# A pool of its own for rounded x, small projection buffers kept open, and a last low part in another buffer

## The chip, the cores and the metric

The kernel runs on one core of a Trainium2 chip. The metric is the device time of one execution in microseconds (us). Six engines matter here: TensorE (PE, with its weight loads PEld), ScalarE (ACT), VectorE (DVE), GpSimd (POOL), SyncE (SP, which only issues transfers) and the 16 DMA engines. ScalarE issues transfers too, on a queue of its own (ACTq in the profile).

## What is computed

```python
x = A_x                                             # 1 x 2048 x 640
g = sigmoid((x * gate_w).sum(-1, keepdims=True))
q, k, v = heads(x @ wqkv)                           # 32 heads of 20
a = softmax(q @ k.T * 20 ** -0.5) @ v               # for each head
a = merge(a) @ wo
h = layernorm(x)                                    # over the 640 channels
u = gelu(einsum("bsd,sf->bdf", h, w1) + b1)         # across the 2048 tokens, F = 1728
b = (einsum("bdf,fs->bds", u, w2) + b2).T
out = g * a + (1 - g) * b
```

## The kernel before

All matrix products run in a three-pass form: each float32 operand is split into a rounded high part and the rest (`hi_lo`: the high part by ScalarE, the low part by VectorE or GpSimd), and high x high, high x low and low x high are added up in PSUM.

The program has these stages, one after the other:

1. Projections. `xh` and `xl` hold all of x, transposed, split into high and low: 20 + 20 tiles of 128 x 512 in the pool `p1` at the right side of the memory. `qk_unit(m, w, q)` makes one 128 x 512 piece of q or k: 15 matmuls, then `evh` (high, ScalarE) and `evl` (low, VectorE), which SyncE's queue stores to DRAM (`q_d`, `k_d`). `evh` and `evl` have two buffers each in `p1`, so each waits for the store of the piece two before it. `p1` also holds two buffers `xr` for raw weights and one `kf` for differences of k, used by the first three column blocks of k alone. Between the pieces, the projections of v and the layernorm statistics are made.
2. The token MLP, in two halves of 320 channels. `w_raw(k)` loads a raw block of weights `wr`, `w_split(k)` splits it into `wh` (ScalarE) and `wl` (GpSimd), and TensorE computes `u` and then `y`. The first four blocks are loaded into `p1` and split into two borrowed tiles `wtmp0`, `wtmp1` while the last projections run; raw blocks 4 to 7 are loaded into other borrowed tiles. From block 4 on the split goes to `wh`/`wl` of the pool `gp`, and from block 8 on the raw blocks go to `wr` of `gp`. `gp` is opened when `p1` is closed and takes its place in the memory. Between the matmuls of the MLP run the score tiles `s` of the first pairs of heads (line 199), of which only the row maxima are kept: by `ov` (ScalarE copies a tile with a Relu, line 214) and then a joint maximum (VectorE, line 224), or by a reduction (line 205).
3. Attention (`st`, exp, `pv`), in which ScalarE's exponentials follow each other closely.
4. The output projection and the gate.

The order on TensorE, ScalarE and VectorE is that of the code from the start, and on GpSimd and SyncE's queue from the MLP's preparation on. In the MLP a small planner with a clock of its own (`act`, `later_on`, `settle`, `force`) decides where ScalarE's steps stand among the others; it knows only its own estimates. The first of its steps is the split of block 4.

The loop `for n, (m, q) in enumerate(units)` (lines 513 to 539) walks the last 24 pieces; n = 20 to 23 are the last four of k, `evh9_0` to `evh9_3` and `evl9_0` to `evl9_3`. Behind it comes `p1s.close()`, line 540.

Of the kernel before, what the change touches and what calls it, by code (L numbers as in the profile page):

```python
# [8 lines left out]
F32R = mybir.dt.float32r  # L9
# [4 lines left out]
P = 128  # L14
# [3 lines left out]
NC = D // P  # L18
# [12 lines left out]
def gated_mix(ctx, tc, xT, x, wqk, wv0, wv1, wo, w1, w1t, b1, w2, b2, out):  # L31
# [6 lines left out]
    def hi_lo(hi, lo, src, hi_eng=None, lo_eng=None):  # L38
        if hi_eng is nc.scalar:
            nc.scalar.activation(hi, src, AF.Copy)  # L40
        else:
            (hi_eng or nc.vector).tensor_copy(hi, src)
        (lo_eng or nc.vector).tensor_sub(lo, src, hi.bitcast(F32))  # L43
# [6 lines left out]
    def mm3(ps, pairs):  # L50
        n = len(pairs)
        for i, (ah, al, bh, bl) in enumerate(pairs):
            for k, (a, b) in enumerate(((ah, bh), (ah, bl), (al, bh))):
                nc.tensor.matmul(ps, a, b, start=(i == 0 and k == 0), stop=(i == n - 1 and k == 2))
# [18 lines left out]
    def st_tile(shape, name):  # L73
        n = st_count[0] % 4
        st_count[0] += 1
        return banks[0].tile(shape, F32, tag=f"st{n}", bufs=1, name=name)
# [12 lines left out]
    def q4(shape, dt, name):  # L89
        return base.tile(shape, dt, tag="q4", bufs=6, name=name)  # L90
# [42 lines left out]
    def base_stack(p, full, eng=nc.sync):  # L133
        ks = k8([P, S], F32R, f"ks{p}_{full}")
        qs = [q4([P, S // 2], F32R, f"qs{p}_{full}_{i}") for i in range(2)]
        load_stack(p, ks, qs, full, eng)
        return ks, qs
# [138 lines left out]

    p1s = ExitStack()
    p1 = p1s.enter_context(tc.tile_pool(name="p1", bufs=1, side="right"))
    xh = [[p1.tile([P, 512], F32R, name=f"xh{c}_{q}") for q in range(4)] for c in range(NC)]
    xl = [[p1.tile([P, 512], F32R, name=f"xl{c}_{q}") for q in range(4)] for c in range(NC)]  # L280

    def w_dma(m):
        raw = p1.tile([P, NC, P], F32, tag="xr", bufs=2, name=f"wr{m}")
# [3 lines left out]
    def load_w(m, raw=None):  # L287
        if raw is None:
            raw = w_dma(m)
        wh = q4([P, NC, P], F32R, f"wh{m}")  # L290
        wl = q4([P, NC, P], F32R, f"wl{m}")
        hi_lo(wh, wl, raw, hi_eng=nc.scalar)
        return wh, wl
# [3 lines left out]
    def qk_unit(m, w, q):  # L297
        wh, wl = w
        ps = st_tile([P, 512], f"qk{m}_{q}")
        mm3(ps, [(wh[:, c], wl[:, c], xh[c][q], xl[c][q]) for c in range(NC)])  # L300
        hi = p1.tile([P, 512], F32R, tag="evh", bufs=2, name=f"evh{m}_{q}")
        lo = p1.tile([P, 512], F32R, tag="evl", bufs=2, name=f"evl{m}_{q}")
        hi_lo(hi, lo, ps, hi_eng=nc.scalar)
        c = m - NC
        dst = q_d if m < NC else k_d
        rows = slice((m % NC) * P, (m % NC + 1) * P)
        cols = slice(q * 512, (q + 1) * 512)
        nc.sync.dma_start(dst[0, rows, cols], hi.bitcast(F32))
        nc.sync.dma_start(dst[1, rows, cols], lo.bitcast(F32))
        if not 0 <= c * P < DROWS:  # L310
            return
        if q % 2 == 0:
            k_first[c] = p1.tile([P, 512], F32, tag="kf", bufs=1, name=f"kf{c}_{q}")
            nc.vector.tensor_copy(k_first[c], ps)
            return
        put = nc.gpsimd.dma_start if c < 2 else nc.sync.dma_start
        put(kd_d[0, rows, cols], hi.bitcast(F32))
        put(kd_d[1, rows, cols], lo.bitcast(F32))
        kd = k_first.pop(c)
        nc.vector.tensor_sub(kd, kd, ps)  # L320
        if c == 2:
            dh = p1.tile([P, 512], F32R, tag="evh", bufs=2, name=f"dh{c}_{q}")
        else:
            dh = (pvp if c else px).tile([P, 512], F32R, tag="dh", bufs=1, name=f"dh{c}_{q}")
        hi_lo(dh, kd.bitcast(F32R), kd, hi_eng=nc.scalar)
        cols = slice((q - 1) * 512, q * 512)
        put(kd_d[0, rows, cols], dh.bitcast(F32))
        put(kd_d[1, rows, cols], kd)
# [18 lines left out]
    w = {0: load_w(0, raws[0])}  # L347
    load_x(0)
    w[NC] = load_w(NC, raws[NC])
    for q in range(4):  # L350
        if q < 3:
            load_x(q + 1)
        if q == 1:
            raws[1] = w_dma(1)
        if q == 2:
            w[1] = load_w(1, raws[1])
            raws[NC + 1] = w_dma(NC + 1)
        qk_unit(0, w[0], q)
        qk_unit(NC, w[NC], q)
# [20 lines left out]
    for n in range(8):  # L380
        if 2 <= n < 2 + NC:
            split_wv(0, n - 2)
            load_wv(1, n - 2)
        qk_unit((1, NC + 1)[n // 4], w[(1, NC + 1)[n // 4]], n % 4)
        if n == 0:
            w[NC + 1] = load_w(NC + 1, raws[NC + 1])
# [13 lines left out]
    for half in range(2):  # L400
        wvh, wvl = wvs[half]
        width = HALF + 2 if half == 0 else HALF
        for t in range(NT):
# [11 lines left out]
            q, cols = t // 4, slice((t % 4) * P, (t % 4 + 1) * P)  # L415
# [26 lines left out]
    def h_load(d, t):  # L442
        xm = hp.tile([P, HALF], F32, tag="xm", bufs=4, name=f"xm{d}_{t}")
        nc.sync.dma_start(xm, x[t * P:(t + 1) * P, d * HALF:(d + 1) * HALF])
        xms[d, t] = xm

    def h_norm(d, t):
        xm = xms[d, t]
        (nc.vector if d else nc.gpsimd).tensor_scalar(xm, xm, negm[:, t:t + 1], rstd[:, t:t + 1], op0=OP.add, op1=OP.mult)

    def h_split(d, t):
        xm = xms.pop((d, t))
        a = hp.tile([P, HALF], F32R, tag=f"hh{t}", name=f"hh{d}_{t}")
        b = hp.tile([P, HALF], F32R, tag=f"hl{t}", name=f"hl{d}_{t}")
        hi_lo(a, b, xm, hi_eng=nc.scalar, lo_eng=nc.gpsimd)
        return a, b
# [14 lines left out]
    def w_raw(k):  # L471
        src, _ = w_list[k]
        n, m = src.shape[1], src.shape[2]
        if k < AHEAD:
            raw = p1.tile([P, 4, P], F32, tag="xr", bufs=2, name=f"wr{k}")
        elif k < 2 * AHEAD:
            raw = q4([P, 4, P], F32, f"wr{k}")
        else:
            raw = gp.tile([P, 4, P], F32, tag="wr", bufs=8, name=f"wr{k}")
        (nc.scalar if k < 2 * AHEAD else nc.sync).dma_start(raw[:, :n, :m], src)  # L480
        w_raws.append(raw)

    def w_split(k):
        src, tail = w_list[k]
        raw = w_raws[k]
        n, m = src.shape[1], src.shape[2]
        if k < AHEAD:
            o = 8 * (k % 2)
            hi, lo = w_tmp[k // 2][:, o: o + 4], w_tmp[k // 2][:, o + 4: o + 8]
        else:  # L490
            hi = gp.tile([P, 4, P], F32R, tag="wh", bufs=5, name=f"wh{k}")
            lo = None if tail else gp.tile([P, 4, P], F32R, tag="wl", bufs=5, name=f"wl{k}")
        if tail:
            hi_lo(hi[:, :n, :m], hi[:, :n, m:], raw[:, :n, :m], hi_eng=nc.scalar, lo_eng=nc.gpsimd)
        else:
            hi_lo(hi[:, :n], lo[:, :n], raw[:, :n], hi_eng=nc.scalar, lo_eng=nc.gpsimd)
        w_got[k] = hi, lo
# [15 lines left out]
    for n, (m, q) in enumerate(units):  # L513
        if q == 0 and n + 4 < len(units):
            w[units[n + 4][0]] = load_w(units[n + 4][0])
        if n == 8:
            s_src[0] = base_stack(0, False, None)
        if 3 <= n < NT + 3:
            hs[n - 3] = h_split(0, n - 3)
        if 2 <= n < NT + 2:  # L520
            h_norm(0, n - 2)
        if 1 <= n < NT + 1:
            h_load(0, n - 1)
        if n == 17:
            w_raw(0)
            w_raw(1)
        if n == 23:
            w_split(3)
        qk_unit(m, w[m], q)
        for _ in range(min(2, len(drip))):  # L530
            drip.pop(0)()
        if n in (18, 19):
            w_split(n - 18)
        if n in (20, 21):
            w_raw(n - 18)
        if n == 22:
            w_split(2)
            w_raw(4)
            w_raw(5)
    p1s.close()  # L540

    gps = ExitStack()
    gp = gps.enter_context(tc.tile_pool(name="gp", bufs=1, side="right"))
# [199 lines left out]
    while done < S_AHEAD:  # L743
        s_next()
        done += 1
    gps.close()
    hps.close()

    ap = ctx.enter_context(tc.tile_pool(name="ap", bufs=1))
# [247 lines left out]
```

## Time and profile before

| | |
|---|---|
| timed runs | 1815.85, 1818.23 and 1818.46 us, median 1818.23 |
| profiled execution | 1813.47 us, its span 1811.7 us |
| projections | 0 to about 218.5 us of the span |
| MLP with score tiles | about 218.5 to 750 us |
| attention | about 750 to 1750 us |
| mean granted TensorE clock | 0.995 |

Times of one row count from the span's first instruction. A row of the timeline gives start, duration, engine, line, operation, output <- inputs, and in brackets the idle time of the engine before it and what ended it. A row of the stretches gives start:end, length, busy time of TensorE with its number of matmuls, the granted TensorE clock, the busy share of the DMA engines and GB/s. A row of the waits gives total, times and the longest.

### The profile page before, as it was taken

The page shows a single profiled execution, that of the slowest core. Times are in us where ns is not written, and L with a number is a line of the kernel's source. Part 1 is how long each engine was busy: PE and PEld are TensorE (multiplying, and loading weights), DVE is VectorE, ACT ScalarE, POOL GpSimd, SP SyncE. Part 2 cuts the span into 40 slices and gives each one's busy share as a digit, 9 for nine tenths or more (in the row PEclk, how much of TensorE's full clock was granted, in tenths as well). Part 3 has the DMA queues.
Part 4 walks back from the last instruction along what each step waited for, and adds up shares of the span by engine and source line. Part 5 has one row for each costly group of instructions (what it writes and reads, how often), then busy time and mean ns, then how long its engine had stood idle before and what let it go on. Part 6 is the DMA issues. An engine that isn't in the chain of part 4 may idle for free. (4 is left out here: it accounts for less than half of the span.)

```text
span 1811.7 us, 39932 instructions
## 1 busy us (share of the span) xinstructions
PE 1787.1 (99%) x14978; PEld 1109.4 (61%) x14978; DVE 1239.9 (68%) x2407; ACT 1484.3 (82%) x2535; POOL 642.5 (35%) x898
## 2 busy tenths in 40 slices
PE   9999889999999999999999999999999999999998
PEld 7998789999999999633333333333333333333378
DVE  5303278899988888867676767676767677777136
ACT  4244278888888887499999999999999999999920
POOL 2113358787878767312111211121331121212210
PEclk9999999999999999999999999999999999999999
DMA  9657867456675555225313232142262323301463
GB/s 303 229 168 238 262 150 185 147 156 201 168 189 164 143 169 163 62 58 138 69 35 76 62 71 63 34 112 61 45 138 60 76 64 64 73 14 23 133 223 134
DMA packets 155666, 222.96 MB, mean 123 GB/s; under 512 B 65998, under 2 KB 92382, under 8 KB 152046
## 3 DMA queue, kind: packets, MB, share of 16 engines
q1 hardware_dynamic: 135472, 186.78, 37.5%
q0 software_dynamic: 15104, 23.01, 5.3%
q10 hardware_dynamic: 4896, 10.62, 1.7%
q8 instruction: 118, 1.93, 0.4%
q14 instruction: 76, 0.62, 0.1%
HBM read 165.43 MB, written 54.54 MB: 121 GB/s over the span
## 5 line engine op out<-in xcount | busy, mean ns | idle before, releaser
L205 DVE TENSOR_REDUCE mx<-s 128x1 f32<-128x512 f32 x1280 | 833.1, 686 | 290.7 <-PE s L199 211.5
L876 ACT ACTIVATE p<-st 128x512 f32<-128x512 f32 x1024 | 570.7, 631 | 0.0
L820 PE MATMUL pv<-p,v 128*32 128x512 f32 x4096 | 549.0, 605 | 0.2 <-DMA sk<-k_d 0.2
L868 ACT ACTIVATE p<-st 128x1024 f32<-128x1024 f32 x512 | 540.0, 1055 | 2.5 <-PE st L861 1.9
L861 PEld LDWEIGHTS st<-qs_True,ks_True 62*128 62x128 f32 x2048 | 246.7, 185 | 436.2 <-ACT p L868 427.3
L861 PE MATMUL st<-qs_True,ks_True 62*128 62x512 f32 x2048 | 496.5, 447 | 1.9 <-ACT x L584 1.1
L199 PE MATMUL s<-ks_False,qs_False 60*128 60x512 f32 x1152 | 393.8, 399 | 11.6 <-ACT ov L214 10.0
L43 POOL TENSOR_TENSOR wl<-wr,wh 128x512 fp32r<-128x512 f32 x228 | 275.6, 1218 | 95.0 <-ACT wh L40 72.0
L224 DVE CUSTOM_DVE_ANT_0 ov<-s,ov 128x512 f32<-128x512 f32 x384 | 263.2, 687 | 42.6 <-PE s L199 25.2
L214 ACT ACTIVATE ov<-s 128x512 f32<-128x512 f32 x384 | 228.9, 598 | 73.0 <-PE s L199 61.5
L199 PE MATMUL s<-sk,sq 60*128 60x512 f32 x896 | 280.3, 394 | 0.0
L807 POOL DMA_DIRECT2D o_d<-oev x128 | 66.7, 521 | 594.9 <-DVE oev L801 592.4
L48 PE MATMUL u<-hl,wh 64*128 64x320 f32 x864 | 226.4, 307 | 0.0
L48 PE MATMUL u<-hh,wh 64*128 64x320 f32 x864 | 226.3, 307 | 0.0
L48 PE MATMUL y<-gh,wh 64*128 64x320 f32 x896 | 225.1, 308 | 0.0
L199 PEld LDWEIGHTS s<-ks_False,qs_False 60*128 60x128 f32 x1152 | 211.2, 185 | 21.9 <-ACT ov L214 10.3
L48 PE MATMUL y<-gl,wh 64*128 64x320 f32 x832 | 216.8, 307 | 0.0
L48 PE MATMUL y<-gh,wl 64*128 64x320 f32 x832 | 215.4, 306 | 0.0
L48 PE MATMUL u<-hh,wl 64*128 64x320 f32 x800 | 214.0, 307 | 0.0
L40 ACT ACTIVATE wh<-wr 128x512 fp32r<-128x512 f32 (+2 forms) x246 | 146.9, 600 | 60.8 <-DMA wr<-in_wqk_dram 25.6
L820 PEld LDWEIGHTS pv<-p,v 128*32 128x32 f32 x4096 | 82.7, 108 | 182.4 <-issue 169.7
L199 PEld LDWEIGHTS s<-sk,sq 60*128 60x128 f32 x896 | 166.0, 186 | 17.9
(130 smaller groups left out, 2436.4 us busy)
## 6 DMA issues: line engine op xcount, KB each, us to landing
wr<-in_w_dram SPq DMA_DIRECT2D x192, 256.0 KB
ks_True<-k_d SPq DMA_DIRECT2D x96, 160.0 KB
qs_True<-q_d SPq DMA_DIRECT2D x192, 80.0 KB
qs_False<-q_d SPq DMA_DIRECT2D x108, 80.0 KB
sk<-k_d SPq DMA_DIRECT2D x42, 160.0 KB
sq<-q_d SPq DMA_DIRECT2D x84, 80.0 KB
v_d<-vt SPq DMA_DIRECT2D x32, 168.0 KB
v<-v_d SPq DMA_DIRECT2D x16, 336.0 KB
```

Source lines behind the costliest of these rows:

```text
L40: nc.scalar.activation(hi, src, AF.Copy)
L43: (lo_eng or nc.vector).tensor_sub(lo, src, hi.bitcast(F32))
L48: nc.tensor.matmul(ps[k], a[r], b[r], start=start, stop=stop)
L199: nc.tensor.matmul(ps, qs[half][r, t * P:(t + 1) * P], ks[r, kc * 512:(kc + 1) * 512], start=True, stop=True)
L205: nc.vector.tensor_reduce(mx[:, slot, j, t: t + 1], ps, axis=AX.X, op=OP.max)
L214: nc.scalar.activation(over[j, kc], ps, AF.Relu)
L224: nc.vector.tensor_tensor_reduce(ov, ps, ov, 1.0, -3.0e38, OP.add, OP.max, mx[:, slot, j, t: t + 1])
L807: nc.gpsimd.dma_start(o_d[DH * h: DH * h + DH, cols], ev[r: r + DH, :])
L820: nc.tensor.matmul(pv[r: r + 32, :], v_tiles[p][:, kt, 10 * j: 10 * j + 32], pt[j, c], start=(kt == 0), stop=(kt == NT - 1))
L861: nc.tensor.matmul(ps, ks[r, kt * P:(kt + 1) * P], qs[qh][r, c * 512:(c + 1) * 512], start=True, stop=True)
L868: nc.scalar.activation(pt, ps, AF.Exp, scale=SCALE)
L876: nc.scalar.activation(pt, ps, AF.Exp, scale=SCALE)
```

## The change

`xh` and `xl` go into a pool `xp` of their own, and that one is closed where `p1` was; `p1`, which keeps `xr`, `evh`, `evl` and `kf`, stays open until the MLP ends. `gp` thus lies where `xh` and `xl` were. The low part of the very last piece goes into the buffer `kf`. The split of block 3 (`w_split(3)`) stands behind the last projection piece and not ahead of it.

```diff
     p1 = p1s.enter_context(tc.tile_pool(name="p1", bufs=1, side="right"))
-    xh = [[p1.tile([P, 512], F32R, name=f"xh{c}_{q}") for q in range(4)] for c in range(NC)]
-    xl = [[p1.tile([P, 512], F32R, name=f"xl{c}_{q}") for q in range(4)] for c in range(NC)]
+    xps = ExitStack()
+    xp = xps.enter_context(tc.tile_pool(name="xp", bufs=1, side="right"))
+    xh = [[xp.tile([P, 512], F32R, name=f"xh{c}_{q}") for q in range(4)] for c in range(NC)]
+    xl = [[xp.tile([P, 512], F32R, name=f"xl{c}_{q}") for q in range(4)] for c in range(NC)]
...
         hi = p1.tile([P, 512], F32R, tag="evh", bufs=2, name=f"evh{m}_{q}")
-        lo = p1.tile([P, 512], F32R, tag="evl", bufs=2, name=f"evl{m}_{q}")
+        tag, bufs = ("kf", 1) if (m, q) == (2 * NC - 1, 3) else ("evl", 2)
+        lo = p1.tile([P, 512], F32R, tag=tag, bufs=bufs, name=f"evl{m}_{q}")
...
+        qk_unit(m, w[m], q)
         if n == 23:
             w_split(3)
-        qk_unit(m, w[m], q)
         for _ in range(min(2, len(drip))):
             drip.pop(0)()
...
-    p1s.close()
+    xps.close()
...
     gps.close()
+    p1s.close()
     hps.close()
```

ScalarE's order around the last projection piece, before. Each row is line, operation, output <- inputs, size, and in brackets the semaphores that it waits for; the numbers behind names only tell buffers apart. `DMAHW0` to `DMAHW7` are eight counters that the transfers of both hardware queues use in turn.

```order
L480 DMA wr4_2151<-in_w1_dram 128x512
L480 DMA wr5_2153<-in_w1_dram 128x512
L40 ACTIVATE wtmp1_1444<-wr3_2125 128x512 [waits DMAHW2_49]
L40 ACTIVATE evh9_3_2173<-qk9_3_2157 128x512 [waits DMAHW3_49,DVE_49,PE_49]
L480 DMA wr6_2185<-in_w1_dram 128x512 [waits DMAHW1_49]
L480 DMA wr7_2187<-in_w1_dram 128x512
L40 ACTIVATE wh4_2193<-wr4_2151 128x512 [waits DMAHW5_49,DMAHW4_49,DMAHW6_49,DMAHW2_49,DMAHW7_49,DVE_49,Pool_49]
L214 ACTIVATE ov0_0_0_1_0_2202<-s0_0_0_1_0_2198 128x512 [waits PE_49]
```

And now:

```order
L483 DMA wr4_2154<-in_w1_dram 128x512
L483 DMA wr5_2156<-in_w1_dram 128x512
L40 ACTIVATE evh9_3_2174<-qk9_3_2158 128x512 [waits DMAHW3_49,DVE_49,PE_49]
L40 ACTIVATE wtmp1_1447<-wr3_2128 128x512 [waits DMAHW2_49]
L483 DMA wr6_2188<-in_w1_dram 128x512
L483 DMA wr7_2190<-in_w1_dram 128x512 [waits DMAHW4_49]
L40 ACTIVATE wh4_2196<-wr4_2154 128x512 [waits DMAHW6_49]
L214 ACTIVATE ov0_0_0_1_0_2205<-s0_0_0_1_0_2201 128x512 [waits PE_49]
```

`evh9_3` and the split of block 3 have changed places. The split `wh4` waited for the stores of `evh9_2`, `evl9_3`, `evh9_3` and `evl9_2`, for its own data `wr4`, for VectorE's `evl9_3` and for GpSimd; it now waits for `wr4` (DMAHW6) alone. The issue of `wr6` no longer waits for the store of `evl9_0`, and that of `wr7` now waits for the store of `evl9_1` (DMAHW4), the last user of the counter that it takes.

SyncE's queue at the same place, before:

```order
L309 DMA k_d_60<-evl9_3_2174 128x512 [waits DMAHW4_49,DVE_49]
L480 DMA wr8_2189<-in_w1_dram 128x512 [waits DMAHW3_49,DMAHW4_49,DMAHW2_49,DMAHW5_49,DMAHW1_49,DMAHW6_49,DMAHW0_49,DMAHW7_49,PE_49,Pool_49]
L480 DMA wr9_2238<-in_w1_dram 128x512 [waits DMAHW6_49]
L480 DMA wr10_2286<-in_w1_dram 128x512
L480 DMA wr11_2331<-in_w1_dram 128x512 [waits DMAHW0_49]
```

And now:

```order
L312 DMA k_d_60<-evl9_3_2175 128x512 [waits DMAHW3_49,DVE_49]
L483 DMA wr8_2192<-in_w1_dram 128x512 [waits DMAHW5_49,PE_49]
L483 DMA wr9_2241<-in_w1_dram 128x512 [waits DMAHW6_49]
L483 DMA wr10_2289<-in_w1_dram 128x512 [waits DMAHW7_49]
L483 DMA wr11_2334<-in_w1_dram 128x512 [waits DMAHW0_49]
```

The order is the same; `wr8` waits for the store of `evh9_2` (DMAHW5) and TensorE's last projection and no longer for all stores and for GpSimd. On VectorE the low part `evl9_3` no longer waits for the store of `evl9_1`; on TensorE and GpSimd the order is unchanged, and the matmuls and low parts on `wh4` have lost the same waits.

## Prediction

> **What bounds the kernel now.** I read the page's busy times first, then the waits of TensorE over the whole span, then the timeline of each engine around the only long wait, and last the busy time by stretches. The page:
>
> ```profile
> span 1811.7 us, 39932 instructions
> PE 1787.1 (99%) x14978; PEld 1109.4 (61%) x14978; DVE 1239.9 (68%) x2407; ACT 1484.3 (82%) x2535; POOL 642.5 (35%) x898
> ```
>
> TensorE (PE) lacks 24.6 us of the span. A part of that is the start and the end; the longest of its waits in between stand here (total, times, longest):
>
> ```profile
> PE s L199 <- ACT ov L214: 10.0, 1, 10.0
> PE a L931 <- DVE oy L935: 2.7, 2, 1.6
> ```
>
> One wait holds 10.0 us, nearly four times the next group. Its place in the timeline, TensorE first, then ScalarE (ACT), VectorE (DVE) and the transfers that SyncE's queue issues:
>
> ```profile
> 220.67 0.39 PE L199 MATMUL s<-ks_False,qs_False 60*128 60x512 f32 x1
> 231.04 0.79 PE L199 MATMUL s<-ks_False,qs_False 60*128 60x512 f32 x1 [9.98 <-ACT ov L214]
> ...
> 217.17 0.33 ACTq L480 DMA_DIRECT2D wr<-in_w_dram  x1
> 219.24 0.96 ACTq L480 DMA_DIRECT2D wr<-in_w_dram  x2
> 222.05 0.63 ACT L40 ACTIVATE wtmp<-wr 128x512 fp32r<-128x512 f32 x1 [1.74 <-DMA wr<-in_w_dram]
> 222.59 0.58 ACT L40 ACTIVATE evh<-qk 128x512 fp32r<-128x512 f32 x1
> 222.80 0.51 ACTq L480 DMA_DIRECT2D wr<-in_w_dram  x1
> 229.88 0.63 ACT L40 ACTIVATE wh<-wr 128x512 fp32r<-128x512 f32 x1 [6.71 <-DMA k_d<-evl]
> 230.41 1.07 ACT L214 ACTIVATE ov<-s 128x512 f32<-128x512 f32 x2
> ...
> 219.98 0.69 DVE L43 TENSOR_TENSOR evl<-qk,evh 128x512 fp32r<-128x512 f32 x1 [1.45 <-DMA k_d<-evl]
> 224.46 0.69 DVE L43 TENSOR_TENSOR evl<-qk,evh 128x512 fp32r<-128x512 f32 x1 [3.79 <-DMA k_d<-evl]
> ...
> 216.32 0.32 SPq L309 DMA_DIRECT2D k_d<-evl  x1
> 218.56 0.32 SPq L309 DMA_DIRECT2D k_d<-evl  x1
> 225.18 0.32 SPq L309 DMA_DIRECT2D k_d<-evl  x1
> 229.92 1.76 SPq L480 DMA_DIRECT2D wr<-in_w_dram  x4
> ```
>
> The chain, read backwards. TensorE stops at 221.06 because its fifth score tile needs a buffer that ScalarE's first `ov` must empty. That `ov` stands behind `wh4` (the first weight split into the MLP's own buffers), which starts only at 229.88. It waits for the last store of the projections, `evl9_3`, issued at 225.18, since `wh4`'s buffer lies in the memory of the pool that held `evl9_3`. That store is late because VectorE made `evl9_3` only at 224.46, after the store of `evl9_1` (issued 218.56) had freed its buffer. From the start of `wh4` to TensorE's restart it is 231.04 - 229.88 = 1.16 us (the split, one `ov`, the hand-over).
>
> The stretches after it (length, TensorE busy, granted clock, DMA share, GB/s) show whether a gain here reaches the end:
>
> ```profile
> 240.50:320.00 79.50, 79.50 (x979) 1.00 0.66 165
> 620.00:750.00 130.00, 129.44 (x1539) 1.00 0.45 133
> 840.00:1600.00 760.00, 760.00 (x5604) 1.00 0.31 69
> ```
>
> TensorE is busy there for 99.6 to 100% and transfers take at most 0.66 of the engines. Nothing follows a clock of its own, so what the stop loses is lost at the end, one for one.
>
> **The change part by part.**
>
> *What `wh4` waits for.* The MLP's pool now takes the place of `xh`/`xl` alone; the projections' small buffers stay. `wh4` then needs three things: ScalarE's turn, the last reader of `xh` (TensorE's last projection, over before the stop), and its own data `wr4`. The seven waits ahead of it shrink to the one for `wr4`, and the store of `evl9_3` no longer matters. What is late next is `wr4`'s landing, which no row shows. It was issued at 219.24. Trips of the neighbours: `wr3` 222.05 - 217.17 = 4.9 us; the stores of `evl9_0` and `evl9_1` 219.98 - 216.32 = 3.7 and 224.46 - 218.56 = 5.9 us. All stores of that tile:
>
> ```profile
> DMA to landing us min/median/max: 3.4/4.9/6.8
> ```
>
> So `wr4` lands between 219.24 + 4.9 = 224.1 and 219.24 + 6.8 = 226.0. The trips grow from 3.7 to 5.9 us within 2.2 us of issue time, and `wr4` is issued 0.7 us after the one of 5.9; I take 6.5, near the upper end: 225.7, and `wh4` at 225.8.
>
> *A new wait ahead of it.* The issue of `wr7` on ScalarE's queue now waits for the store of `evl9_1` (the counter that it reuses). Behind it on ScalarE stand `wh4` and every `ov`, and TensorE waits for those. It ends at 224.46, the issue takes 0.51 (row at 222.80): 224.97, hidden by `wr4` by 0.8 us. If `wr4` came at 224.1 this wait would set `wh4`. So `wh4` starts at 224.97 at the earliest and 226.1 at the latest, 3.8 to 4.9 us earlier than now; I take 229.88 - 225.8 = 4.1 us.
>
> *Low part in the differences' buffer.* `evl9_3` no longer waits for a store; it comes right after `evh9_3`, about 1.5 us earlier, and so does its store. VectorE's next reduction comes earlier too, but TensorE waits for `ov`, not for it: nothing.
>
> *The third `wtmp1` split behind the last unit's evacuation.* ScalarE swaps two instructions; no transfer is issued by either, and the split moves back by one instruction of about 0.6 us, GpSimd's low half with it (to about 225). TensorE needs that weight in the last quarter of `u0_0`, which ended with
>
> ```profile
> 240.46 0.31 PE L48 MATMUL u<-hh,wh 64*128 64x320 f32 x1
> ```
>
> 9.4 us after the restart; its last quarter begins several us behind the restart, in the changed kernel not before 231. If that cover were gone the price would be those 0.6 us.
>
> *SyncE's queue.* `wr8` to `wr11`, issued in one row at 229.92 behind `evl9_3`'s landing, now wait each for one earlier transfer and come up to 4 us sooner. They are needed after `wh4` to `wh7`: no gain of their own. Closing the small pool at the end of the MLP adds no instruction; from there on the orders are the same, and so are the waits, but for a few of TensorE's on loads that landed long before.
>
> *The clock.* Rows at edges of the clock's steps (length, TensorE busy, clock):
>
> ```profile
> 218.09:221.51 3.42, 2.97 (x26) 1.00 0.89 295
> 221.51:224.92 3.41, 0.00 (x0) 1.00 0.81 231
> 224.92:228.33 3.41, 0.00 (x0) 0.50 0.99 371
> 228.33:231.75 3.42, 0.71 (x4) 0.50 0.28 77
> 231.75:235.16 3.41, 3.41 (x27) 0.50 0.91 283
> 235.16:238.57 3.41, 3.41 (x46) 1.00 0.70 138
> ...
> 753.99:757.40 3.41, 1.82 (x12) 1.00 0.16 53
> 757.40:760.82 3.42, 3.25 (x16) 0.50 0.63 156
> 760.82:764.23 3.41, 3.41 (x26) 1.00 0.65 157
> ```
>
> The clock falls to 0.50 and comes back only at multiples of 3.413 us: (757.40 - 224.92) / 3.413 = 156.0. A step that is 53% busy (753.99) is followed by 0.50, one that is 87% busy (218.09) by 1.00. After the stop TensorE runs at half speed from 231.04 to 235.16, 4.12 us, which costs 2.06. With a stop of 9.98 - 4.1 = 5.9 us there is always a step with over 1 us idle, so the clock falls all the same. TensorE restarts at 226.94; on the same grid the step from 224.92 is 1.39 / 3.41 = 41% busy, too little, so full speed returns at 231.75: 4.81 us at half speed, 2.41 lost, 0.35 more than now. On other grids, with a limit somewhere between 53 and 87%, the half-speed time is 1.8 to 6.4 us (0.9 to 3.2 us lost), and with the limit in the middle (70%) its mean is 3.41 x 1.2 = 4.1 us, what it is now. The runs behind the median need not share the profile's grid, so I take 0 for this term and -1.2 to +1.1 as its ends.
>
> The Trainium skill ("TensorE: Matmul & The Clock Gate", Part 1) says that the activity window of 3.4 us runs freely and that the half rate comes after at least one idle window. The grid agrees with that, 3.413 us in the rows; that the window must be idle does not: the one at 753.99 was 53% busy. By the page's rule some grids would keep the clock up, which is a rival below.
>
> **Sum.** The profiled execution took 1813.47 us (span 1811.7 and 1.8 around it). Stop shorter: -4.1; clock: 0; the rest: 0. That is 1809.4 for an execution like the profiled one. The three timed runs lie higher, 1815.85 to 1818.46, with a median of 1818.23; the same difference gives 1818.23 - 4.1 = 1814.1 us, 0.23% less. About 0.2%, 3.6 us, is what a measurement of this kernel can tell from no change, so the forecast stands barely beyond it.
>
> **The rivals.**
>
> *Smaller, within 0.2%.* `wr4` lands at 226.0 or the clock's grid falls badly (up to 1.1 us more lost). Then 2.6 us remain: 1815.6. For it: trips are still growing at 219, and on the profile's own grid the clock term is +0.35. Against: both ends together are needed to come much below 3.
>
> *The clock stays up.* If only a wholly idle step lowers the clock, a stop of 5.9 us contains none on (2 x 3.41 - 5.9) / 3.41 = 27% of the grids, and the 2.06 us at half speed go too: -6.2, 1812.0. Against: the row at 753.99, and the profile's own step from 221.51 would still be idle.
>
> *Slower: the stop comes back at `wh6`/`wh7`.* `wr7` is issued about 2 us later than now, and `wr8` onwards earlier, so they compete. ScalarE's splits `wh6` and `wh7` stand ahead of `ov` just as `wh4` does:
>
> ```profile
> 236.49 0.63 ACT L40 ACTIVATE wh<-wr 128x512 fp32r<-128x512 f32 x1
> 237.66 0.62 ACT L40 ACTIVATE wh<-wr 128x512 fp32r<-128x512 f32 x1
> ```
>
> Moved up by 4.1, `wh7`'s turn comes at 233.6; `wr7`, issued at 224.5, has 9.1 us until then. From that trip on each microsecond stops TensorE again, and a stop over about 1 us brings another 2.06 at half clock. Slower by 3.6 needs 4.1 + 3.6 - 2.06 = 5.6 us of stop, a trip of 14.7 us: about 1821.9. For it: DMA is 0.99 busy at 224.92. Against: the longest trip of the tile above is 6.8, and DMA falls to 0.28 busy from 228.33.
>
> **How the numbers follow.** Forecast (1814.1): 0.52. Smaller (1815.6): 0.33. Clock stays up (1812.0): 0.09. Slower (1821.9): 0.06. Faster by over 0.2%: 0.52 + 0.09 = 0.61; within: 0.33; slower: 0.06. The range reaches down to the clock rival with 1 us for the spread of the runs, 1811.0, and up to the smaller gain with its clock end and some spread, 1817.0; the slower case and the tails are left out.
>
> **What would show it.** Right: `wh4` starts near 225.8, released by `wr4`'s transfer and not by a store of `evl`; the one long wait of TensorE falls from 10.0 to about 5.9 us; the clock still falls once there; all later stages have their lengths. Wrong: `wh4` later than 226.9 (a wait I have not seen), a new wait of ScalarE at `wh5` to `wh7`, no fall of the clock, or a later stage that grows by what was won.

## The result and the profile after

The changed kernel took 1809.94 us (median of 9 runs, 1807.24 to 1814.68), the kernel before beside it 1817.25 us (9 runs, 1815.85 to 1820.28). The ratio is 0.9966, with a 95% interval of 0.9956 to 0.9977: 6.2 us less (4.2 to 8.0). The two medians lie 7.3 us apart; I go by the ratio, which is taken over all runs. The profiled execution took 1807.24 us and was the fastest of the nine. Its page:

```profile
span 1804.9 us, 39919 instructions
...
PE 1787.0 (99%) x14978; PEld 1117.5 (62%) x14978; DVE 1240.6 (69%) x2407; ACT 1483.9 (82%) x2535; POOL 641.8 (36%) x898
```

TensorE's work is what it was (1787.1 before), but it now lacks 17.9 us of the span where it lacked 24.6. Its waits (total, times, longest):

```profile
PE a L935 <- DVE oy L939: 3.0, 2, 1.8
PE s L199 <- ACT ov L214: 2.9, 1, 2.9
```

The wait for the score copies `ov` has gone from 10.0 to 2.9 us, and a wait of the output stage now stands above it. The same place in the timeline, TensorE, then ScalarE, VectorE and SyncE's queue:

```profile
223.68 0.49 PE L199 MATMUL s<-ks_False,qs_False 60*128 60x512 f32 x1 [2.85 <-ACT ov L214]
232.78 0.31 PE L48 MATMUL u<-hh,wh 64*128 64x320 f32 x1
...
216.03 0.60 ACT L40 ACTIVATE evh<-qk 128x512 fp32r<-128x512 f32 x1 [1.34 <-DMA k_d<-evh]
216.08 1.21 ACTq L483 DMA_DIRECT2D wr<-in_w_dram  x2
220.69 0.90 ACTq L483 DMA_DIRECT2D wr<-in_w_dram  x1
222.51 0.63 ACT L40 ACTIVATE wh<-wr 128x512 fp32r<-128x512 f32 x1 [1.72 <-DMA wr<-in_w_dram]
...
220.30 0.69 DVE L43 TENSOR_TENSOR evl<-qk,evh 128x512 fp32r<-128x512 f32 x1 [0.77 <-ACT evh L40]
...
221.05 0.56 SPq L312 DMA_DIRECT2D k_d<-evl  x1
```

`wh4` is released by its own data `wr4` and no longer by the last store of the projections, although that store was issued only 1.5 us ahead (221.05 and 222.51). `evl9_3` waits only for `evh9_3` now. But one thing differs that the change does not touch: the evacuation `evh9_2`, right behind which `wr4` is issued, starts at 216.03. Before it stood here:

```profile
219.20 0.60 ACT L40 ACTIVATE evh<-qk 128x512 fp32r<-128x512 f32 x1 [1.45 <-DMA k_d<-evh]
```

So TensorE's restart, 231.04 before and 223.68 now, moved by 7.36 us in two parts: 3.17 us because this evacuation came earlier, and 4.20 us because `wh4` follows it after 6.48 us (222.51 - 216.03) and no longer after 10.68 (229.88 - 219.20). Only the second has to do with the waits of `wh4`. I use this reading for all runs below: from the start of `evh9_2`'s evacuation to `wh4`, and from there to the restart, which is 1.16 to 1.17 us each time that `wh4` stands ahead of the first `ov`.

The stretches at the edges of the clock's steps (length, TensorE busy, clock, DMA share, GB/s), at this place and in the output stage:

```profile
221.26:224.67 3.41, 0.99 (x12) 1.00 0.93 332
224.67:228.09 3.42, 3.42 (x28) 0.50 0.97 294
...
1747.02:1750.43 3.41, 1.64 (x11) 1.00 0.84 321
1750.43:1753.84 3.41, 3.38 (x13) 0.50 0.90 307
```

The clock fell here for one step, 3.41 us at half speed against 4.12 before: 0.35 us saved. The first matmul on a `wh` of the MLP comes at 232.78 instead of 240.46, 7.68 us earlier, which is 7.36 + 0.35 within 0.03. How it reaches the end shows in the exponentials (counts, durations in ns, first and last start), before and now:

```profile
L868 ACT ACTIVATE p<-st x512: 1024/1032/1187, 755.5 to 1727.8; 128x1024 f32<-128x1024 f32 x171
```

```profile
L872 ACT ACTIVATE p<-st x512: 1023/1043/1187, 747.7 to 1718.5; 128x1024 f32<-128x1024 f32 x171
```

The first one starts 7.8 us earlier, the last one 9.3, the span ends 6.8 earlier. Attention took 970.8 us instead of 972.3: before, the clock fell once at its start (757.40). The output stage took 86.4 us from the last of these rows instead of 83.9, with the fall at 1750.43. This holds over all thirteen profiles of this study: attention takes 972.1 to 972.3 us in the five in which the clock fell at its start and 970.8 to 971.0 in the other eight; the output stage takes 85.5 to 87.2 us in the eight with such a fall in it (between 1750 and 1763) and 83.9 to 85.2 in the five without.

### The profile page after: what moved, and what is told of

It is laid out like the page before. It is cut to its first block, busy times and chain, and to the rows that moved or that the text cites. A ratio compares the mean times of both kernels' runs of the same rounds, so it can differ in the third digit from the quotient of the medians.

```text
span 1804.9 us, 39919 instructions
## 1 busy us (share of the span) xinstructions
PE 1787.0 (99%) x14978; PEld 1117.5 (62%) x14978; DVE 1240.6 (69%) x2407; ACT 1483.9 (82%) x2535; POOL 641.8 (36%) x898
## 5 line engine op out<-in xcount | busy, mean ns | idle before, releaser
L880 ACT ACTIVATE p<-st 128x512 f32<-128x512 f32 x1024 | 585.1, 659 | 0.0
L872 ACT ACTIVATE p<-st 128x1024 f32<-128x1024 f32 x512 | 553.8, 1082 | 1.3 <-PE st L865 0.7
```

The lines of the kernel that those rows point to most:

```text
L872: nc.scalar.activation(pt, ps, AF.Exp, scale=SCALE)
L880: nc.scalar.activation(pt, ps, AF.Exp, scale=SCALE)
```

## Experiments

**The two kernels again.** One profile of each can't tell what the waits brought (4.2 us) from what may have come by chance (3.2), so both were run again without an edit. Of before:

> The kernel before once more, for a second profile and the spread of a ratio of equals. Theory A with transfers that vary: a ratio of 1.000 within 0.1%, and a stop that differs from 10.0 us by 1 us or more, with the stores of the last pieces landing that much earlier or later. Rival (fixed by the program): 10.0 within 0.3.

Measured: 0.9998 (0.9987 to 1.0009), median 1816.66 us.

```profile
232.23 0.79 PE L199 MATMUL s<-ks_False,qs_False 60*128 60x512 f32 x1 [10.23 <-ACT ov L214]
...
220.18 0.60 ACT L40 ACTIVATE evh<-qk 128x512 fp32r<-128x512 f32 x1 [1.43 <-DMA k_d<-evh]
231.06 0.63 ACT L40 ACTIVATE wh<-wr 128x512 fp32r<-128x512 f32 x1 [6.35 <-DMA k_d<-evl]
...
227.29 0.32 SPq L309 DMA_DIRECT2D k_d<-evl  x1
```

From evacuation to `wh4` it takes 10.88 us, where the first profile had 10.68. The stop is 10.23 us, 0.25 from the first one and not 1 or more as I had expected, although the evacuation starts 0.98 us later. Of the changed kernel, with the first four experiments:

> The changed kernel once more, for a second profile. Theory A with transfers that vary from one execution to the next: the stop lies between 2 and 7 us, and its end is 1.2 us behind the start of the first MLP split, which is released by a weight transfer; the ratio to before is 0.996 to 0.998. Rival (the stop is fixed by the program): 2.9 us again within 0.3.

Measured: 0.9965 (0.9953 to 0.9978), median 1810.46 us.

```profile
223.16 0.49 PE L199 MATMUL s<-ks_False,qs_False 60*128 60x512 f32 x1 [1.22 <-ACT ov L214]
...
216.41 0.60 ACT L40 ACTIVATE evh<-qk 128x512 fp32r<-128x512 f32 x1 [1.78 <-DMA k_d<-evh]
222.00 0.63 ACT L40 ACTIVATE wh<-wr 128x512 fp32r<-128x512 f32 x1 [0.50 <-DMA wr<-in_w_dram]
```

```profile
223.20:227.00 3.80, 3.80 (x48) 1.00 0.93 313
```

5.59 us to `wh4`, a stop of 1.22 us, below the 2 us that I had expected at least, and no fall of the clock behind it. This profiled execution, too, was the fastest of its series (1807.04 of six). And a third time, on another chip, beside the last two experiments:

> The changed kernel a third time, beside the two others of this call and for a third profile. Theory A: a ratio of 0.996 to 0.9975; from the start of the evacuation of the last piece but one (the issue of block 4's load) to the first MLP split 5 to 6.7 us as in the other profiles with the pools apart, where the kernel before has 10.7 to 10.9, wherever in the execution that evacuation falls.

Measured: 0.9983 (0.9973 to 0.9993), median 1814.72 us, which is 3.1 us less than before. This interval does not hold the first two ratios, and the ratio lies above the 0.9975 that I had expected at most.

```profile
229.52 0.79 PE L199 MATMUL s<-ks_False,qs_False 60*128 60x512 f32 x1 [6.27 <-ACT ov L214]
...
221.16 0.60 ACT L40 ACTIVATE evh<-qk 128x512 fp32r<-128x512 f32 x1 [2.22 <-DMA k_d<-evh]
227.97 0.34 ACTq L483 DMA_DIRECT2D wr<-in_w_dram  x1
228.35 0.63 ACT L40 ACTIVATE wh<-wr 128x512 fp32r<-128x512 f32 x1 [2.39 <-DMA wr<-in_w_dram]
```

```profile
227.19:230.60 3.41, 1.08 (x7) 0.50 1.03 285
230.60:234.02 3.42, 3.42 (x27) 0.50 0.72 138
```

```profile
L872 ACT ACTIVATE p<-st x512: 1023/1043/1187, 754.1 to 1726.4; 128x1024 f32<-128x1024 f32 x171
```

Here the evacuation came at 221.16, 5 us later than in the other two, and `wh4` 7.19 us behind it, more than the 6.7 that I had expected at most; the stop is 6.27 us, and half speed lasts 4.50 us behind it. The whole execution, 1815.70 us, is 2.2 us longer than the profiled one of before, although the first exponential starts 1.4 us earlier: from the last one to the end of the span it takes 87.1 us, where before took 83.9. The output stage varies by that much without the change: in the thirteen profiles of this study it took 83.9 to 87.2 us, and both ends belong to kernels with the old pools; the clock fell in it here, at 1759.78, and not in the first profile of before.

Over the profiles, the way from evacuation to `wh4` is 10.68 and 10.88 us before, 6.48, 5.59 and 7.19 after: means 10.8 and 6.4, a gain of 4.4 us (3.5 to 5.3 by single pairs). When the evacuation itself starts shows no tie to the pools: 216.03 to 223.22, on average 219.8, in the nine of kernels with the new pools, and 219.20 to 221.77, on average 220.4, in the four with the old ones.

**One half of the change: the pools alone.** From the changed kernel:

```diff
-        tag, bufs = ("kf", 1) if (m, q) == (2 * NC - 1, 3) else ("evl", 2)
-        lo = p1.tile([P, 512], F32R, tag=tag, bufs=bufs, name=f"evl{m}_{q}")
+        lo = p1.tile([P, 512], F32R, tag="evl", bufs=2, name=f"evl{m}_{q}")
...
-        qk_unit(m, w[m], q)
         if n == 23:
             w_split(3)
+        qk_unit(m, w[m], q)
```

> Of the change only the pools: the low part of the last piece stays in its own pair of buffers and the split of block 3 stays ahead of the last evacuation. Theory A (where the first MLP weight buffers lie decides; the wait for the last stores goes, the landing of its own data is what is left): all of the gain within 1 us, so about 6 us less than the kernel before, a stop of TensorE of 3 to 6 us, the first MLP split released by a weight transfer. Theory B (the low part's own buffer and the order carry it, since they bring the last store forward): less than half of the gain, under 3 us.

Measured: 0.9971 (0.9958 to 0.9984), median 1810.37 us.

```profile
226.35 0.79 PE L199 MATMUL s<-ks_False,qs_False 60*128 60x512 f32 x1 [4.84 <-ACT ov L214]
...
220.18 0.60 ACT L40 ACTIVATE evh<-qk 128x512 fp32r<-128x512 f32 x1 [2.00 <-DMA k_d<-evh]
225.18 0.63 ACT L40 ACTIVATE wh<-wr 128x512 fp32r<-128x512 f32 x1 [1.99 <-DMA wr<-in_w_dram]
```

5.00 us to `wh4`, and a stop of 4.84, within the expected 3 to 6. The pools alone bring what the whole change brings, as far as the intervals tell.

**The other half: buffer and order alone.** From the kernel before, the two hunks above the other way round:

```diff
-        lo = p1.tile([P, 512], F32R, tag="evl", bufs=2, name=f"evl{m}_{q}")
+        tag, bufs = ("kf", 1) if (m, q) == (2 * NC - 1, 3) else ("evl", 2)
+        lo = p1.tile([P, 512], F32R, tag=tag, bufs=bufs, name=f"evl{m}_{q}")
...
+        qk_unit(m, w[m], q)
         if n == 23:
             w_split(3)
-        qk_unit(m, w[m], q)
```

> The other two parts alone: the low part of the last piece in the differences' buffer and the split of block 3 behind the last evacuation, with the pools as before. Theory A: the first MLP split still waits for the last store, which is made about 1.5 us earlier (its low part no longer waits for a store), so 1 to 2 us less than before and a stop of 8 to 9 us. Theory B: 4 us less or more.

Measured: 1.0003 (0.9994 to 1.0012), median 1817.51 us. The expected gain of 1 to 2 us did not come, and the stop is 9.38 us, not 8 to 9.

```profile
221.77 0.60 ACT L40 ACTIVATE evh<-qk 128x512 fp32r<-128x512 f32 x1 [1.50 <-DMA k_d<-evh]
232.58 0.63 ACT L40 ACTIVATE wh<-wr 128x512 fp32r<-128x512 f32 x1 [6.32 <-DMA k_d<-evl]
...
225.77 0.69 DVE L43 TENSOR_TENSOR evl<-qk,evh 128x512 fp32r<-128x512 f32 x1 [1.48 <-ACT evh L40]
...
226.51 0.91 SPq L310 DMA_DIRECT2D k_d<-evl  x1
```

The last store is issued 4.74 us behind `evh9_2`'s evacuation (226.51 - 221.77), 1.24 us sooner than before (225.18 - 219.20 = 5.98). It lands no sooner: `wh4` comes 10.81 us behind the evacuation, as before. From the issue to `wh4` it takes 6.1 us, where it took 4.7. One reason stands in the traces' counter events (the moments at which a transfer's counter rises, which no row above shows): `wh4` waits for the store of `evh9_3` as well, and before that one was complete at 229.21 and the store of `evl9_3` at 229.65, so moving the second alone could bring 0.4 us at most. Here they were complete at 231.95 and 232.35.

**Where does the rest of the stop come from: the order on ScalarE.** If `wh4`'s wait stops TensorE only because the first `ov` stand behind it, `ov` ahead of `wh4` should do as much. On the changed kernel, the planner learns that block 4 comes 2 us later, which puts two `ov` ahead of its split:

```diff
-            act(lambda: w_split(j), 520, 0, 2200 * (j - k) - 4000)
+            act(lambda: w_split(j), 520, 2000 if j == AHEAD else 0, 2200 * (j - k) - 4000)
```

> The changed kernel with the first MLP split (block 4) behind the first two score copies on ScalarE instead of ahead of them (its ready time in the planner 2000 ns later). Theory A (ScalarE's order makes a weight transfer hold up TensorE; the split's result is needed some 9 us after the restart): the stop ends with the last evacuation and the issue of block 7's load, not with block 4's landing: 1 to 2 us shorter, so 1 to 2 us less than the changed kernel, up to 3.5 less if the clock then stays up. Rival: the split comes too late for the second u tile or the first copies wait on something else: no gain or a loss.

Measured: 0.9955 (0.9943 to 0.9966), median 1809.71 us. The interval overlaps those of the changed kernel, so the gain of 1 to 2 us over it is not shown, and the stop in the profile, 5.51 us, is no shorter.

```profile
227.76 0.79 PE L199 MATMUL s<-ks_False,qs_False 60*128 60x512 f32 x1 [5.51 <-ACT ov L214]
...
226.73 0.33 ACTq L483 DMA_DIRECT2D wr<-in_w_dram  x1
227.11 1.09 ACT L214 ACTIVATE ov<-s 128x512 f32<-128x512 f32 x2 [2.44 <-DMA k_d<-evl]
```

The `ov` is first in line, but the issue of `wr7` stands ahead of it on ScalarE and waits for the store of `evl9_1` until 226.73. That is the new wait that the prediction named, here in the open. With the loads of blocks 6 and 7 on SyncE's queue as well:

```diff
-        (nc.scalar if k < 2 * AHEAD else nc.sync).dma_start(raw[:, :n, :m], src)
+        (nc.scalar if k < 6 else nc.sync).dma_start(raw[:, :n, :m], src)
```

> As the run before, and the loads of blocks 6 and 7 issued by SyncE's queue, so that on ScalarE nothing that waits for a store stands ahead of the first score copies but the last evacuation itself. Theory A: the stop ends about 1.7 us behind the start of the last evacuation (two splits, a copy, the hand-over): another 0.5 to 2 us off. Rival: the weight loads come late on the other queue, and ScalarE waits at the splits of blocks 6 and 7.

Measured: 0.9949 (0.9933 to 0.9965), median 1808.24 us; not to be told from the run without this edit.

```profile
226.70 0.50 PE L199 MATMUL s<-ks_False,qs_False 60*128 60x512 f32 x1 [4.17 <-ACT ov L214]
...
225.04 0.60 ACT L40 ACTIVATE evh<-qk 128x512 fp32r<-128x512 f32 x1 [2.94 <-DMA k_d<-evh]
```

Now `ov` follows the last evacuation `evh9_3`, which itself waits 2.94 us for a store; TensorE restarts 1.66 us behind its start, as expected. Each wait taken from the head of ScalarE's queue uncovers the next one.

**Is there slack at this place.** On the changed kernel, 15 unused matmuls (some 3.5 us) between the projections and the MLP; they add work whose result is not used:

```diff
+    fill = st_tile([P, 512], "fill")
+    for i in range(15):
+        ks, qs = s_src[0]
+        nc.tensor.matmul(fill, qs[0][:3 * DH, :P], ks[:3 * DH, :512], start=True, stop=True)
     xps.close()
```

> The changed kernel with 15 more matmuls (3.5 us, their result unused) between the last projection and the MLP. Theory A (transfers set the end of the stop, the clock falls for idle steps): the stop shrinks by about 3.5 us where it is that long, the restart stays where it was, and what is at stake is the half-speed time: between 2 us less and 1 us more than the changed kernel. Rival (TensorE's own work is what counts there): 3.5 us more.

Measured: 0.9966 (0.9953 to 0.9979), median 1810.32 us: 3.5 us more of TensorE's work cost nothing that can be measured. In the profile the fifteen matmuls take 3.69 us, `wh4` comes 6.74 us behind the evacuation (229.96 and 223.22), as without them, and 3.16 us of the stop are still left. What TensorE does there lies under ScalarE's wait.

**Is the wait for `wr4` a matter of its issue.** On the changed kernel, `wr4` and `wr5` one piece earlier:

```diff
-        if n == 22:
-            w_split(2)
+        if n == 21:
             w_raw(4)
             w_raw(5)
+        if n == 22:
+            w_split(2)
```

> The changed kernel with the loads of blocks 4 and 5 issued one projection piece (3.5 us of TensorE's time) earlier. Theory A (the landing of block 4 ends the stop): the first MLP split starts 1 to 2 us earlier, less than the 2 to 3 us of the issue since the queue is full; 1 to 2 us less than the changed kernel. Rival (queue full: the load only pushes the stores back, and the last evacuation waits for these): no gain, or up to 2 us more.

Measured: 0.9969 (0.9957 to 0.9981), median 1812.74 us: no gain.

```profile
225.05 0.79 PE L199 MATMUL s<-ks_False,qs_False 60*128 60x512 f32 x1 [2.92 <-ACT ov L214]
...
222.82 0.60 ACT L40 ACTIVATE evh<-qk 128x512 fp32r<-128x512 f32 x1 [3.10 <-DMA k_d<-evh]
223.88 0.63 ACT L40 ACTIVATE wh<-wr 128x512 fp32r<-128x512 f32 x1
```

`wh4` comes 5.27 us behind `evh9_2`'s evacuation (218.61) and no longer waits for a transfer, but it stands behind `evh9_3`, which waited 3.10 us for its buffer. That wait takes the place of the other.

**All of them out of the way.** The edits of the last ScalarE pair, and the last evacuation and the split of block 3 made steps of the planner as well, due some microseconds later:

```diff
+    def qk_evac(m, q, ps):
...
-            act(lambda: w_split(j), 520, 0, 2200 * (j - k) - 4000)
+            act(lambda: w_split(j), 520, {4: 4500, 5: 3000}.get(j, 0), 2200 * (j - k) - 4000)
...
-        qk_unit(m, w[m], q)
-        if n == 23:
-            w_split(3)
+        qk_unit(m, w[m], q, last_evac if n == 23 else None)
...
+    act(lambda: w_split(3), 520, 2600, 1500)
+    act(last_evac[0], 600, 3600, 2000)
```

> The changed kernel with ScalarE's order mended further: the loads of blocks 6 and 7 on SyncE's queue, and the split of block 3, the evacuation of the last projection piece and the split of block 4 each behind the first three score copies or later. Theory A (what stops TensorE is a wait for transfers at the head of ScalarE's queue, ahead of score copies that need none): the first stop falls below 1 us, a short one may come at the last evacuation; 2 to 5 us less than the changed kernel, a ratio to before of 0.993 to 0.9955. Rival (the waits only move on: block 3, the last store or block 4 stop TensorE a few us later for as long): the ratio of the changed kernel, 0.9965.

Measured: 0.9942 (0.9929 to 0.9955), median 1806.72 us, the fastest of all; the changed kernel on the same chip had 1814.72, and the two intervals do not meet (0.9973 to 0.9993 there). They also hardly meet those of the first two measurements, which begin at 0.9956 and 0.9953. TensorE's waits for `ov`:

```profile
PE s L199 <- ACT ov L214: 2.2, 3, 1.1
```

Three waits of 1.1 us at most are left.

**The same gain without the change.** From the kernel before, with its pools as they were: only the order on ScalarE and the queue of two loads.

```diff
-        (nc.scalar if k < 2 * AHEAD else nc.sync).dma_start(raw[:, :n, :m], src)
+        (nc.scalar if k < 6 else nc.sync).dma_start(raw[:, :n, :m], src)
...
-            act(lambda: w_split(j), 520, 0, 2200 * (j - k) - 4000)
+            act(lambda: w_split(j), 520, {4: 6000, 5: 4000}.get(j, 0), 2200 * (j - k) - 4000)
```

> The kernel before, its pools, buffers and its order of the last piece kept, with only ScalarE's planner changed: the splits of blocks 4 and 5 are ready 6000 and 4000 ns later, so that five score copies stand ahead of the first split into the MLP's pool, and the loads of blocks 6 and 7 go through SyncE's queue. Theory A: the wait for the last stores is still there (the first such split starts near 230), but TensorE restarts some 2 us behind the last evacuation, near 224.5, and stops again for 1 to 3 us; 3 to 5 us less than before without any buffer moved. Rival (the memory itself is what matters): no gain over before, within 0.1%.

Measured: 0.9961 (0.9947 to 0.9974), median 1810.55 us, 7.1 us less than before and more than the 3 to 5 expected, on the chip of the third measurement of the changed kernel (1814.72). The two edits were not tried apart.

```profile
223.95 0.50 PE L199 MATMUL s<-ks_False,qs_False 60*128 60x512 f32 x1 [1.57 <-ACT ov L214]
227.24 0.79 PE L199 MATMUL s<-ks_False,qs_False 60*128 60x512 f32 x1 [2.05 <-DVE mx L205]
...
225.90 0.69 DVE L43 TENSOR_TENSOR evl<-qk,evh 128x512 fp32r<-128x512 f32 x1 [4.29 <-DMA k_d<-evl]
...
231.43 0.62 ACT L40 ACTIVATE wh<-wr 128x512 fp32r<-128x512 f32 x1
```

`wh4` starts as late as ever, at 231.43 (11.15 us behind the evacuation at 220.28), and TensorE no longer stops for it. Of the stop, 1.57 us are left for the first `ov` and 2.05 for VectorE's reduction behind `evl9_3`, whose wait for a buffer is still there in these pools.

## Why the prediction was right, and where it was not

The sign and the mechanism were right; 1814.1 us was 4.2 too high, and 1809.94 lies 1.1 below the range that I gave. The kernel before ran faster beside it than in the three runs that I forecast from; from their 1818.23 the ratio gives 1812.0, 2.1 below the forecast and inside the range. The three ratios of the changed kernel stand for -6.2, -6.4 and -3.1 us, on average -5.2.

*What `wh4` waits for.* Right, and shown twice over: the pools alone bring the gain (0.9971), and before with `ov` ahead of `wh4` (and two loads on the other queue) brings it too (0.9961), so it was the place of that wait ahead of `ov` that stopped TensorE. The size was near: I took 4.1 us, with `wr4` landing at 225.7; over the profiles it is 4.4, with 6.48, 5.59 and 7.19 us from evacuation to `wh4`. No row showed `wr4`'s landing, but the counter events of the trace of before have it complete at 225.74.

*The step that failed* is the one that carried the times of one profile over as fixed: "issued at 219.24", so `wh4` "at 225.8". In the thirteen profiles the evacuation `evh9_2`, which `wr4` follows in all but the one with the earlier load, starts anywhere from 216.03 to 223.22. In the first profile after, `wh4` came at 222.51, below the 224.97 that I had as its earliest; with the 6.48 us of that profile and the evacuation where it was before, it would have come at 219.20 + 6.48 = 225.68, as predicted. So -6.2 us in the first measurement has some 4.4 in it that the waits account for; the rest is not accounted for by a step of mine, and I can't show that the change causes it. The third measurement, with 3.1, lies on the other side. The average of the three, -5.2, is near the 4.4 and the half microsecond of the clock below.

*The rest: 0.* This term was a little too low. An execution lasts 1.7 to 1.9 us longer than its span in all runs with the old pools and 2.0 to 2.4 us longer in all with the new ones, so the change costs some 0.4 us there; the runs do not show why.

*The new wait.* "Hidden by `wr4` by 0.8 us" was too sure. In the third profile `wr7`'s issue ends its wait 0.4 us ahead of `wh4` and is itself over at 228.31, 0.04 ahead; by the counter events `wr4` was complete at 228.12, so there the new wait came last, by 0.2 us. And as soon as `ov` was put ahead of `wh4` it held the stop at 5.51 us.

*Low part and split order: nothing.* Right: 1.0003 for both without the pools. (The row at 240.46, which the prediction gives as the end of `u0_0`, is the first matmul of the next tile; nothing hangs on it.) In the experiment I expected one to two microseconds of them, and was wrong there.

*The clock.* Its term of 0 holds on average (2.06 and 1.49 us lost before, from 4.12 and 2.97 us at half speed; 1.70, 0 and 2.25 after), a difference of about -0.5 within the ends of -1.2 to +1.1. That the clock falls "all the same" was wrong in one of three profiles, since I had assumed a stop of 5.9 us, and it was 1.22 there. The limit for the fall, which I put somewhere between 53 and 87% busy, lies at 50 to 57% in the profiles (see the last section).

*The rivals.* The slower one did not occur: no wait at `wh5` to `wh7` shows among TensorE's waits, and the first `wh` matmul keeps the whole 7.36 us. The clock rival's number, 1812.0, is what the first ratio gives, nearer than my forecast, but that is luck: in two of three profiles the clock fell behind the stop all the same. Within 0.2% (-3.6 us) is where the third measurement fell, so the chance of 0.33 for that was not idle.

*What stays open.* Why the transfers ahead of this place run earlier or later from one execution to the next (by 5 us in the three profiles of the changed kernel, by 2.6 in three with the old pools) was not found; the evacuations wait for stores each time (1.3 to 2.2 us in the rows above), so it is the stores that come early or late. Nor is it settled why the third measurement gave half the gain. Its profile is 8.6 us of span longer than the first one, and the parts can be read: 5.1 from the later evacuation, 0.7 from there to `wh4`, 0.5 from half speed behind the restart, 1.5 from a fall of the clock at the start of attention and 0.7 from the output stage. Such differences go with the clock: of the 26 executions of the changed kernel, the four with a mean granted clock of 0.998 took 1808.0 us on average, the four with 0.995 or less 1815.3. Whether the chip, which was another one too, plays a part was not tried.

## What to carry to other kernels

When an engine that works in order has a wait for a transfer at the head of its queue, all that stands behind it waits too: look at what the next engine needs of that queue, and put that ahead. Memory that is taken over brings the waits of everything that used it, also of transfers that have nothing to do with the new owner; giving the buffers with late stores a place that nobody takes over (0.9971) and changing the order together with the queue of two loads (0.9961) each brought the gain alone here, 0.3 to 0.4%, though neither removed the whole stop. And a place that is costed from one profile should be read in a second one first: here its times moved by as much as the gain.

## What the runs showed that I had not expected

When the last store was issued did not set when `wh4` could start: 4.74, 5.98 and 7.11 us behind the same evacuation in three profiles with the old pools (the second of before: 227.29 - 220.18), with `wh4` 10.81, 10.68 and 10.88 us behind it. The DMA engines were 0.81 and 0.99 busy in the two steps from 221.51 before, so transfers already under way may be what sets the landing; no run changed how many these are, so that is not shown.

The clock fell behind a step that was 48% busy (1.64 of 3.41 us, at 1747.02), as it had behind one of 53% before the change. Over the thirteen profiles, no step at full speed that was over 57% busy was followed by half speed (1.96 of 3.42 us, third profile of the changed kernel, at 752.84), and the emptiest that kept full speed was 50% busy (1.70 of 3.41, second profile of before, at 1754.13). In between the busy share alone does not decide. To come back took more: behind a step at half speed that was 78% busy (2.65 of 3.42, the pools alone, at 225.58) the clock stayed down, behind one of 87% (2.97 of 3.42, second profile of before, at 231.78) it rose. The Trainium skill ("TensorE: Matmul & The Clock Gate", Part 1) gives the half rate after at least one idle window; here windows that were half busy were enough, and these rows decide.
